# Attention and two expert layers in one kernel: new start places in SBUF for the Relu quarters and the weight slots

## The chip, the cores and the metric

One Trainium2 chip (trn2), one of its NeuronCores. The metric is the device time of one execution in microseconds (us); lower is better. "Place" means the byte at which an operand begins within a partition of SBUF, and "remainder" means that place modulo 256.

## What is computed

The reference runs linear attention with an RMS norm, then a dense layer of eight experts (every token goes through all eight, weighted by a balanced gate `P`), then a layer of eight experts in which each token goes to its best one:

```python
# dense expert layer, x: 2304 x 512, w1: 8 x 512 x 1024, w2: 8 x 1024 x 512
for e in range(E):
    h = np.maximum(x @ w1[e], 0.0)
    ye = h @ w2[e]
    out += P[:, e:e + 1] * ye
...
# routed expert layer
for e in range(E):
    mask = expert_idx == e
    h = np.maximum(x[mask] @ w1[e], 0.0)
    out[mask] = gate_w[mask, None] * (h @ w2[e])
```

## The kernel before, in words

Each fp32 matrix is held as a high and a low part in a reduced fp32 format (`F32R`). A product is three matmuls: high by high, high by low, low by high. Every matmul is one weight load of a 128x128 block (the stationary operand) and one pass of 256, 384 or 512 columns of the other operand (the moving one).

The dense layer is 24 steps: three blocks of 768 tokens times eight experts. The first matrix of a step is done with seven products of quarters in place of eight, in `fill` (L967): stationary is a weight quarter, moving is a quarter of the tokens (`xo`), 384 columns. That is 168 matmuls in each of the 24 steps, 4032 in all. Its results go through Relu and are kept as four "Relu quarters", each with a high and a low part of 1536 elements, named 11, 12, 21 and 22 and held in two tiles (in the profile all of them are called `d`).

The second matrix comes in two kinds. In steps 8 to 22 (`quick`) it is done with seven products of quarters, in `product` inside `down` (L1103): stationary is a Relu quarter, moving is a weight quarter, 256 columns; 252 matmuls in each of 15 steps, 3780 in all. In the steps 0 to 7 it is done in the plain way (L1316): the same stationary operands, moving weights of 512 columns, 1152 matmuls. The last step has its own code (L1344, 144 matmuls of 512 columns). The routed layer follows, with `f1` (L593, 256 columns), `f2` (L613, 512 columns, moving operand in the weight slots) and `single` (L1536, L1561, 512 columns).

Weights pass through four slots. Quarter number `g` of the whole program goes to slot `g % 4`, a high and a low tile of 4096 bytes. `slot_tiles` makes the two tiles anew for each quarter. They are filled in one of two ways: ScalarE casts the high part and GpSimd or VectorE subtracts it to make the low one (`prep`, `split_into`, L161, L166, L260), or SyncE fetches both parts from a copy in HBM (`fetch`, L279). Quarter `g + 3` is asked for while quarter `g` is being used (`ahead`).

The order of all work is written out by hand; nothing is scheduled by a planner. What the tiles' addresses are follows from their sizes and the order of the pools. Before the change all eight slot tiles begin at remainder 160, the token parts `xo` at 224, and the Relu tiles at 160; `place_h` moves the Relu quarters by 16 elements (64 bytes) in the fast steps, so that they begin at 224 there, and leaves them at 160 in the others. Quarters and rows within them are multiples of 256 bytes apart, so each matmul of a kind begins its two operands at the same two remainders: 160 (stationary) and 224 (moving) in `fill`, 224 and 160 in the fast steps' second matrix, 160 and 160 in the plain one and in `f2`, 160 and 96 in `f1` (its first call 224 and 160), 96 and 160 in `single`.

Of the kernel before, what the change touches and what calls it, by code (L numbers as in the profile page):

```python
# [9 lines left out]
F32R = mybir.dt.float32r  # L10
# [7 lines left out]
N, D, E, F = B * S, H * HD, 8, 1024  # L18
P = 128
# [21 lines left out]
def f32(ap):  # L41
    return ap.bitcast(F32)

@with_exitstack
def tile_linattn_moe_moe(ctx: ExitStack, tc: tile.TileContext, qT, k, v, g2, wg, w1a, w2a, emb, embT, tau, w1b, w2b, out):
# [4 lines left out]
    wp = ctx.enter_context(tc.tile_pool(name="w", bufs=1))  # L50
# [9 lines left out]
    def get(pool, shape, dtype, tag, bufs=1):  # L60
        if not ringed[0]:
            return pool.tile(shape, dtype, tag=tag, name=tag, bufs=bufs)
        if tag not in rings:
            rings[tag] = [[pool.tile(shape, dtype, tag=tag, name=tag, bufs=bufs) for _ in range(bufs)], 0]
        r = rings[tag]
        r[1] += 1
        return r[0][(r[1] - 1) % bufs]
# [84 lines left out]

    def split(raw, tag, eng=None, hi_eng=None):
        pool, name = places[tag]
        hi = get(pool, [P, 1024], F32R, name + "h")
        lo = get(pool, [P, 1024], F32R, name + "l")
        return split_into(raw, hi, lo, eng, hi_eng)

    def split_into(raw, hi, lo, eng=None, hi_eng=None):
        if hi_eng is None:  # L160
            nc.scalar.copy(hi, raw)  # L161
        else:
            hi_eng.tensor_copy(hi, raw)
        if eng is nc.gpsimd and dense[0]:
            for c in (slice(0, 512), slice(512, 1024)):
                eng.tensor_tensor(lo[:, c], raw[:, c], f32(hi[:, c]), ALU.subtract)  # L166
        else:
            (eng or nc.vector).tensor_tensor(lo, raw, f32(hi), ALU.subtract)
        return hi, lo
# [19 lines left out]
    def quick(s):  # L189
        return E <= s < NSTEP - 1  # L190
# [9 lines left out]
    for i, g in enumerate(plain):  # L200
        plain_load.setdefault(plain[i - 2] - 2 if i > 1 else base[E] - 4 + i, []).append(g)

    def slot_tiles(g):
        return (wp.tile([P, 1024], F32R, tag=f"g{g % 4}h", name="wh", bufs=1),
                wp.tile([P, 1024], F32R, tag=f"g{g % 4}l", name="wl", bufs=1))

    def load_quarter(s, name, t=None):
        t = t if t is not None else raw_tile()
# [34 lines left out]
    def prep(g, lo_eng=None):  # L243
        s, n = seq_of[g]

        def r(name):
            return raws[s, name]

        if g in plain_at:
            src = raws[g]  # L250
        elif n >= 7:
            src = r(W2ORDER[n - 7])
        else:
            if n == 2 and s == 0:
                sums(s)
            src = r(("w11", "w12", "s2", "w21", "w22", "s1", "w12")[n])
        hi, lo = parts[g] = slot_tiles(g)
        if s < E and lo_eng is None and g > 2:
            nc.scalar.copy(hi, src)  # L259
            after_two.append([2, lambda: nc.vector.tensor_tensor(lo, src, f32(hi), ALU.subtract)])  # L260
        else:
            split_into(src, hi, lo, lo_eng)
        if s < E and n in (2, 3):
            o, a, b = (r(i) for i in (("w21", "w11", "w21"), ("w12", "w12", "s2"))[n - 2])
            for c in (slice(0, 512), slice(512, 1024)):
                nc.gpsimd.tensor_tensor(o[:, c], a[:, c], b[:, c], ALU.subtract)
# [7 lines left out]
    def fetch(g):  # L274
        s, n = seq_of[g]
        parts[g] = slot_tiles(g)
        src = w1c[s % E, CACHED[n]] if n < 7 else w2c[s % E, DOWN[n - 7][1]].rearrange("i p f d -> i p (f d)")
        for i in range(2):
            nc.sync.dma_start(f32(parts[g][i]), src[i])  # L279
# [285 lines left out]
    xrow = qs.rearrange("p k n -> p (k n)")  # L565
    hq = {}
    groups = []
    HSHIFT = 16

    def place_h(o):  # L570
        for names, t in groups:
            for i, a in enumerate(names):
                hq[a] = [t[:, o + k * 4 * HB:o + (k + 1) * 4 * HB].rearrange("p (k n) -> p k n", k=4)
                         for k in (2 * i, 2 * i + 1)]

    def open_h(pool, names):
        groups.append((names, pool.tile([P, 16 * HB + HSHIFT], F32R, name="d" + names[0])))
        place_h(0)
# [620 lines left out]
    for s in range(NBK * E):  # L1199
# [28 lines left out]
                               (a + 20, lambda r: t_store(r, 0)), (a + 24, lambda r: t_store(r, 1))):  # L1228
                    thooks.setdefault(min(at_, 311), []).append(lambda f=f, r=r: f(r))
        fast = quick(s)  # L1230
        place_h(HSHIFT if fast else 0)
        if final:
            raw_n[0] = 0
        bank = {}
# [2 lines left out]
        for n in range(7):  # L1237
            g = base[s] + n
# [67 lines left out]
        elif not final:  # L1306
            ys = [ps_a() for _ in range(JT)]
            for m, q in enumerate(W2ORDER):
                g = base[s] + 7 + m
                wh, wl = parts[g]  # L1310
# [281 lines left out]
    def slot(f):  # L1592
        if f in steps:
            steps[f]()
        if f < 4:
            w2t.append(split(early2[f], f"w2{f}", nc.gpsimd))
        if f < 2:
            early_w1(f + 2, 1)
        if f == 1:
            for j in range(FT // 2):  # L1600
                early_w2(j, 1)
# [10 lines left out]
    def mid(f):  # L1612
        if f == 1:
            q_count()
        if f == 4:
            q_experts()
        kk = {1: 0, 3: 1}.get(f)
        if kk is not None:
            w1t[kk] = split(next1[kk], f"w1{kk}")
# [5 lines left out]
    def mid(f):  # L1625
        if f in (0, 2):
            kk = 3 - f // 2
            w1t[kk] = split(next1[kk], f"w1{kk}")
        if f == 3:
            q_slot()  # L1630
        if f == 6:
            q_cols(A16, R16, 0, NA)
# [166 lines left out]
```

## Time and profile before

| | |
|---|---|
| median of 3 runs | 1821.28 us (1820.44 to 1821.89) |
| the profiled execution | 1820.02 us |
| its span, first to last instruction | 1818.2 us |
| TensorE matmul busy (PE) | 1788.0 us, 98% |
| TensorE weight load busy (PEld) | 1698.3 us, 93% |
| VectorE, ScalarE, GpSimd busy (DVE, ACT, POOL) | 68%, 47%, 56% |
| granted TensorE clock | 0.995 of full, the 2.4 GHz level |

A row of instructions gives line, engine, operation, output and inputs by the program's names, the shape, a count, busy time and the mean duration of one. Matmuls overlap: a matmul's duration in the profile is longer than the time from its start to the next one's start. That second time, the spacing, is what adds up to the span.

### The profile page before, as it was taken

How to read it: one execution, taken by the hardware profiler on the slowest of the kernel's cores; microseconds unless marked ns; L12 is line 12 of the kernel's file. 1: busy time of each engine (PE TensorE's matmuls, PEld its weight loads, DVE VectorE, ACT ScalarE, POOL GpSimd, SP SyncE). 2: the span in 40 equal slices, each digit the busy share in tenths (PEclk: the TensorE clock that was granted, in tenths of full speed). 3: DMA queues.
4: the chain of work that ended last, by engine and by line, in shares of the span. 5: the costliest groups of instructions: out<-in, count | busy, mean ns of one | idle time of the engine just before them, and what ended most of it. 6: DMA issues, size and time to landing. Idle time of an engine off the chain costs nothing. (4 is left out here: it accounts for less than half of the span.)

```text
span 1818.2 us, 30973 instructions
## 1 busy us (share of the span) xinstructions
PE 1788.0 (98%) x11494; PEld 1698.3 (93%) x11494; DVE 1243.3 (68%) x2196; ACT 847.2 (47%) x1435; POOL 1021.7 (56%) x813
## 2 busy tenths in 40 slices
PE   7999999999999999999999999999999999999997
PEld 7989889989998999999999999999999998888996
DVE  3855686566656788866456778987567764877665
ACT  3645344344434634554444553454445433556443
POOL 1513378889879655764466475765466432543222
PEclk9999999999999999999999999999999999999998
DMA  9625367779768766556465766565555663588764
GB/s 298 224 70 203 106 227 277 259 268 342 277 233 280 273 212 211 197 186 223 167 217 190 247 220 237 179 216 208 181 198 186 228 212 102 188 304 287 232 227 157
DMA packets 185568, 397.73 MB, mean 219 GB/s; under 512 B 16448, under 2 KB 86592, under 8 KB 185408
## 3 DMA queue, kind: packets, MB, share of 16 engines
q1 hardware_dynamic: 179680, 378.33, 60.4%
q0 software_dynamic: 4000, 13.11, 2.1%
q10 hardware_dynamic: 1728, 4.23, 0.7%
q8 instruction: 92, 1.51, 0.3%
q14 instruction: 68, 0.56, 0.1%
HBM read 314.61 MB, written 81.00 MB: 218 GB/s over the span
## 5 line engine op out<-in xcount | busy, mean ns | idle before, releaser
L967 PE MATMUL A<-xo,wh 128*128 128x384 f32 x2688 | 687.8, 337 | 1.0 <-DVE u L955 0.4
L967 PEld LDWEIGHTS A<-xo,wh 128*128 128x128 f32 x2688 | 482.6, 188 | 3.2 <-DVE u L955 1.2
L967 PE MATMUL A<-xo,wl 128*128 128x384 f32 x1344 | 452.2, 336 | 1.8 <-POOL wl L166 1.4
L1103 PE MATMUL A<-wh,d 128*128 128x256 f32 x2520 | 447.7, 281 | 0.6 <-POOL d L1157 0.6
L166 POOL TENSOR_TENSOR wl<-raw,wh 128x512 fp32r<-128x512 f32 x180 | 254.4, 1435 | 285.4 <-ACT wh L161 129.0
L1103 PEld LDWEIGHTS A<-wh,d 128*128 128x128 f32 x2520 | 387.6, 190 | 0.8 <-POOL d L1157 0.8
L1103 PE MATMUL A<-wl,d 128*128 128x256 f32 x1260 | 353.7, 281 | 0.0
L967 PEld LDWEIGHTS A<-xo,wl 128*128 128x128 f32 x1344 | 252.6, 188 | 3.3 <-POOL wl L166 2.6
L1316 PE MATMUL A<-wh,d 128*128 128x512 f32 x768 | 243.8, 392 | 0.0
L1103 PEld LDWEIGHTS A<-wl,d 128*128 128x128 f32 x1260 | 236.5, 188 | 0.0
L952 DVE SCALAR_TENSOR_TENSOR d<-A,d 128x384 fp32r<-128x384 f32 x228 | 125.9, 553 | 160.4 <-ACT raw L1254 90.1
L166 POOL TENSOR_TENSOR wl<-rb,wh 128x512 fp32r<-128x512 f32 x92 | 129.3, 1426 | 161.4 <-ACT wh L161 150.2
L1316 PEld LDWEIGHTS A<-wh,d 128*128 128x128 f32 x768 | 144.2, 188 | 29.7 <-issue 0.3
L957 ACT ACTIVATE d<-A 128x384 fp32r<-128x384 f32 x132 | 65.4, 497 | 198.5 <-DVE A L955 196.2
L1316 PE MATMUL A<-wl,d 128*128 128x512 f32 x384 | 149.5, 389 | 0.0
L1250 ACT COPY qs<-A 128x384 f32<-128x384 f32 x96 | 45.5, 479 | 190.1 <-PE A L967 185.4
L161 ACT CAST wh<-raw 128x1024 fp32r<-128x1024 f32 x94 | 98.4, 1047 | 12.4 <-DMA raw<-in_w1a_dram 4.2
L260 DVE TENSOR_TENSOR wl<-raw,wh 128x1024 fp32r<-128x1024 f32 x45 | 70.3, 1564 | 36.4 <-ACT wh L259 25.8
L1153 POOL TENSOR_TENSOR d<-qs,d 128x384 fp32r<-128x384 f32 x60 | 64.8, 1111 | 48.0 <-ACT d L1151 48.0
L1316 PEld LDWEIGHTS A<-wl,d 128*128 128x128 f32 x384 | 72.2, 188 | 14.1
L955 DVE TENSOR_TENSOR A<-A,qs 128x384 f32<-128x384 f32 x132 | 73.6, 560 | 16.7 <-PE A L967 16.4
L1259 DVE TENSOR_TENSOR u<-A,qs 128x384 f32<-128x384 f32 x96 | 52.2, 554 | 32.0 <-PE A L967 31.9
(496 smaller groups left out, 3366.6 us busy)
## 6 DMA issues: line engine op xcount, KB each, us to landing
raw<-in_w1a_dram SPq DMA_DIRECT2D x64, 512.0 KB, 4.4
wh<-w1c SPq DMA_DIRECT2D x64, 512.0 KB, 4.9
wl<-w1c SPq DMA_DIRECT2D x64, 512.0 KB, 6.4
wh<-w2c SPq DMA_DIRECT2D x60, 512.0 KB, 5.1
wl<-w2c SPq DMA_DIRECT2D x60, 512.0 KB, 5.9
raw<-in_w2a_dram SPq DMA_DIRECT2D x51, 512.0 KB, 4.5
raw<-in_w1b_dram SPq DMA_DIRECT2D x48, 512.0 KB, 5.0
raw<-in_w2b_dram SPq DMA_DIRECT2D x48, 512.0 KB, 3.8
```

Of the source, the lines that this page charges most:

```text
L161: nc.scalar.copy(hi, raw)
L166: eng.tensor_tensor(lo[:, c], raw[:, c], f32(hi[:, c]), ALU.subtract)
L260: after_two.append([2, lambda: nc.vector.tensor_tensor(lo, src, f32(hi), ALU.subtract)])
L952: nc.vector.scalar_tensor_tensor(hl[:, i, :], src, 0.0, f32(hh[:, i, :]), ALU.max, ALU.subtract)
L955: nc.vector.tensor_tensor(dst, ps, u, ALU.add)
L957: nc.scalar.activation(hq[a][0][:, i, :], dst, AF.Relu)
L967: nc.tensor.matmul(ps[:, 0:HB], a[:, fs], bb[:, kk, :], start=(first and j == 0), stop=(j == 5), skip_group_check=True)
L1103: nc.tensor.matmul(o, a[:, f, ts_], bb[:, ds_], start=(m in first and j != 1 and i == 0), stop=(i == 11), skip_group_check=True)
L1153: nc.gpsimd.tensor_tensor(a12[1][:, i], qs[:, i], f32(a12[0][:, i]), ALU.subtract)
L1250: nc.scalar.copy(qs[:, i, :], p)
L1259: nc.vector.tensor_tensor(u3[:, i, :], p, qs[:, i, :], ALU.add)
L1316: nc.tensor.matmul(ys[j], a, bb[:, ds_], start=(m + ff + i == 0), stop=(m == 3 and ff == 1 and i == 2))
```

## The change

Three edits. (1) The four weight slots become four tiles that are made once, each of 2048 + 16 elements; the high part begins the tile, and the low part begins 0, 8, 4 or 16 elements (0, 32, 16, 64 bytes) behind the end of the high one. As a tile is now 64 bytes longer, the slots begin at remainders 160, 224, 32 and 96, and their low parts at 160, 0, 48 and 160. (2) In the fast step `s` the Relu quarters are placed `2 * (s - 8)` elements into their tiles, that is 0, 8, 16 ... 112 bytes, in place of 64 bytes in all of them. (3) The Relu tiles grow by 16 elements (64 bytes) to hold that; one of them stays at 160 and the other, which is laid out from the far end, comes to begin at 96. `split` takes the slots' parts directly for the second expert layer.

```diff
     def split(raw, tag, eng=None, hi_eng=None):
         pool, name = places[tag]
+        if pool is wp:
+            return split_into(raw, *slots[int(name[1])], eng, hi_eng)
...
+    slots = {}
+    LOW_AT = (0, 8, 4, 16)
+
     def slot_tiles(g):
-        return (wp.tile([P, 1024], F32R, tag=f"g{g % 4}h", name="wh", bufs=1),
-                wp.tile([P, 1024], F32R, tag=f"g{g % 4}l", name="wl", bufs=1))
+        if g % 4 not in slots:
+            o = 1024 + LOW_AT[g % 4]
+            t = wp.tile([P, 2048 + 16], F32R, name=f"g{g % 4}")
+            slots[g % 4] = t[:, 0:1024], t[:, o:o + 1024]
+        return slots[g % 4]
...
-    HSHIFT = 16
+    HSHIFT = 32
...
-        place_h(HSHIFT if fast else 0)
+        place_h(2 * (s - E) if fast else 0)
```

No instruction is added, removed or moved on any engine; lines move by 8. What differs in the program are addresses, the names of the slot tiles (now `g` for both parts), and which semaphores some instructions wait for. GpSimd, in a fast step's second matrix, before (`wl` and `wh` are a slot's parts, `rb` and `raw` hold plain weights, `d` is a Relu quarter):

```order
L166 TENSOR_TENSOR wl<-rb,wh 128x512 [waits DMAHW4_49,DMAHW6_49,PE_49,Activation_49]
L166 TENSOR_TENSOR wl<-rb,wh 128x512
L1273 TENSOR_TENSOR d_766<-u_518,d_766 128x384 [waits Activation_49] x2
L166 TENSOR_TENSOR wl<-raw,wh 128x512 [waits DMAHW1_49,PE_49,Activation_49]
L166 TENSOR_TENSOR wl<-raw,wh 128x512
```

and the same place after the change:

```order
L168 TENSOR_TENSOR g_566<-rb,g_566 128x512 [waits DMAHW5_49,DMAHW0_49,Activation_49]
L168 TENSOR_TENSOR g_566<-rb,g_566 128x512 [waits PE_49]
L1281 TENSOR_TENSOR d_756<-u_515,d_756 128x384 [waits Activation_49] x2
L168 TENSOR_TENSOR g_500<-raw,g_500 128x512 [waits DMAHW1_49,Activation_49]
L168 TENSOR_TENSOR g_500<-raw,g_500 128x512 [waits PE_49,Pool_49]
```

The wait for TensorE moves from the first half of a low part to the second half, as the halves are now tracked apart; the instructions and their order are the same.

## Rows read from the trace of the kernel before

**Rows 1.** The page, part 1, and the granted clock of part 2.
```profile
PE 1788.0 (98%) x11494; PEld 1698.3 (93%) x11494; DVE 1243.3 (68%) x2196; ACT 847.2 (47%) x1435; POOL 1021.7 (56%) x813
...
PEclk9999999999999999999999999999999999999998
```
**Rows 2.** Who waited for whom, TensorE: us in total, times, longest.
```profile
PE M L381 <- DMA v<-in_v_dram: 7.3, 2, 5.8
...
PE A L967 <- POOL wl L166: 1.4, 3, 0.8
...
PE A L1103 <- POOL d L1157: 0.6, 1, 0.6
```
**Rows 3.** The page, part 5, the three large matmul groups with `wh`.
```profile
L967 PE MATMUL A<-xo,wh 128*128 128x384 f32 x2688 | 687.8, 337 | 1.0 <-DVE u L955 0.4
...
L1103 PE MATMUL A<-wh,d 128*128 128x256 f32 x2520 | 447.7, 281 | 0.6 <-POOL d L1157 0.6
...
L1316 PE MATMUL A<-wh,d 128*128 128x512 f32 x768 | 243.8, 392 | 0.0
```
**Rows 4.** Timeline of TensorE in a fast step, 17 triples apart: start us, us.
```profile
868.86 0.40 PE L1103 MATMUL A<-wh,d 128*128 128x256 f32 x2
...
874.87 0.40 PE L1103 MATMUL A<-wh,d 128*128 128x256 f32 x2
```
**Rows 5.** Groups of TensorE, 912 to 941.4 us (second matrix, step 13).
```profile
L1103 PE MATMUL A<-wh,d 128*128 128x256 f32 x167 | 29.6, 281 | 0.0
L1103 PE MATMUL A<-wl,d 128*128 128x256 f32 x84 | 23.6, 281 | 0.0
```
**Rows 6.** Timeline of TensorE in step 21, around a small matmul group.
```profile
1397.93 0.28 PE L1103 MATMUL A<-wh,d 128*128 128x256 f32 x1
1398.06 0.46 PE L810 MATMUL M<-pG,pB 128*128 128x6 bf16 x12
1398.38 0.36 PE L1103 MATMUL A<-wh,d 128*128 128x256 f32 x1
```
**Rows 7.** Groups of TensorE, 1399.2 to 1405.3 us (step 21, after that group).
```profile
L1103 PE MATMUL A<-wh,d 128*128 128x256 f32 x38 | 6.5, 276 | 0.0
L1103 PE MATMUL A<-wl,d 128*128 128x256 f32 x19 | 5.2, 276 | 0.0
```
**Rows 8.** Timeline of TensorE there, 16 triples apart.
```profile
1399.61 0.28 PE L1103 MATMUL A<-wl,d 128*128 128x256 f32 x1
...
1405.05 0.28 PE L1103 MATMUL A<-wl,d 128*128 128x256 f32 x1
```
**Rows 9.** Groups of TensorE in `f1`, 1631 to 1642, then 1780 to 1795 us.
```profile
L593 PE MATMUL A<-xh,w13h 128*128 128x256 f32 x7 | 1.9, 276 | 0.0
...
L593 PE MATMUL A<-xh,w10h 128*128 128x256 f32 x8 | 2.2, 281 | 0.0
```
**Rows 10.** By line, whole span: duration ns min/median/max, first and last start us.
```profile
L967 PE MATMUL A<-xo,wl x1344: 332/336/445, 54.1 to 1502.1; 128*128 128x384 f32 x192
...
L1103 PE MATMUL A<-wl,d x1260: 276/281/283, 618.0 to 1472.9; 128*128 128x256 f32 x180
...
L1316 PE MATMUL A<-wl,d x384: 387/389/397, 96.2 to 587.6; 128*128 128x512 f32 x192
```
**Rows 11.** Groups of TensorE, 95.8 to 136 us (rows often broken).
```profile
L967 PE MATMUL A<-xo,wl 128*128 128x384 f32 x1 | 0.3, 338 | 0.0
```
**Rows 12.** By line, `single` (stationary at 96, moving at 160), and `f2` (160 and 160).
```profile
L1536 PE MATMUL A<-w10h,xh x4: 392/392/392, 1618.0 to 1657.2; 128*128 128x512 f32 x4
...
L1536 PE MATMUL A<-w10l,xh x4: 394/394/394, 1618.2 to 1657.4; 128*128 128x512 f32 x4
...
L1536 PE MATMUL A<-w10h,xl x4: 388/388/388, 1618.5 to 1657.7; 128*128 128x512 f32 x4
...
L613 PE MATMUL A<-g0l,hh x40: 389/389/398, 1557.7 to 1803.6; 128*128 128x512 f32 x40
```
**Rows 13.** Timeline of GpSimd in step 12, then of TensorE at the same place.
```profile
876.33 2.57 POOL L166 TENSOR_TENSOR wl<-rb,wh 128x512 fp32r<-128x512 f32 x2
...
874.04 0.28 PE L1103 MATMUL A<-wl,d 128*128 128x256 f32 x1
```
**Rows 14.** Timelines of GpSimd, then VectorE, end of step 15 and step 16.
```profile
1051.61 5.35 POOL L1157 TENSOR_TENSOR d<-raw,d 128x384 fp32r<-128x384 f32 x4
...
1070.39 0.56 DVE L952 SCALAR_TENSOR_TENSOR d<-A,d 128x384 fp32r<-128x384 f32 x1 [0.81 <-ACT raw L1254]
```
**Rows 15.** The page, part 6: fetches into the slots, KB each, us to landing.
```profile
wl<-w1c SPq DMA_DIRECT2D x64, 512.0 KB, 6.4
...
wl<-w2c SPq DMA_DIRECT2D x60, 512.0 KB, 5.9
```

## The prediction

> **What bounds the kernel now.** I read the page's busy times first. TensorE's matmuls are busy for 1788.0 of 1818.2 us and the clock is granted in full in every slice that counts [rows 1]; the other engines are well below. The waits of TensorE come next: the longest total is 7.3 us at the first loads, and the two largest inside the dense layer are 1.4 and 0.6 us [rows 2]. So there is no wait left from which a change of order could take much. What remains is how long one matmul takes, times their number. The matmul groups give the numbers [rows 3]: 4032 matmuls of 384 columns (2688 with `wh`, half as many with `wl`), 3780 of 256 columns in the fast steps, 1152 of 512 columns in the plain ones.
>
> A matmul's duration in these rows is not its cost; the spacing to the next start is. In a settled stretch of a fast step, 17 triples take 874.87 - 868.86 = 6.01 us, or 117.8 ns a matmul [rows 4], where the mean duration is 281 ns [rows 5]. Duration less spacing is 163 ns. I take this constant for the other settled stretches: 336 ns of duration at 384 columns is a spacing of 173 ns, and 389 ns at 512 columns is 226 ns [rows 10]. A nanosecond more or less in the duration is then a nanosecond of span for each matmul of that group.
>
> From 384 to 512 columns the duration grows by 53 ns, 0.414 ns a column, which is a cycle at 2.4 GHz (0.417 ns). At that rate 256, 384 and 512 columns are 106.7, 160.0 and 213.3 ns. So each matmul pays about 11, 13 and 13 ns beyond its columns. This extra is nearly the same for 384 and 512 columns, so it belongs to the one weight load that goes with each matmul and not to the columns. That is the only thing this change can touch.
>
> **Does it depend on the place?** The trace holds three hints.
> - At one shape, one line and one pair of remainders it takes two values: 281 ns in most fast products, 276 ns after a short group of other matmuls had broken the row [rows 6, 7]; the spacing there is 5.44 us over 48 matmuls, 113.3 ns [rows 8]. `f1` shows the same two values [rows 9]. Matmul and weight load thus settle into a fixed pattern, and there is more than one such pattern.
> - Where stationary and moving operand stand in another relation, the pattern is another: `single` (96 and 160) repeats 392, 394, 388, a mean of 391.3 ns, against 389 ns for `f2` (160 and 160), both at 512 columns [rows 12]. That is 2.3 ns more.
> - While a row is unsettled, durations spread from 332 to 338 ns at 384 columns (the 445 is the break itself) and from 387 to 397 ns at 512 [rows 10, 11].
>
> So a weight load's extra can be moved, by some nanoseconds either way, and the place is one of the things that go with it.
>
> The Trainium skill speaks against this: TensorE: Matmul & The Clock Gate, Part 2 (Step-by-step), says that the engine reads the streamed operand and the weights through two independent ports, so that loading the next weights takes nothing from the running matmul; then no place could matter. The trace does not agree with it as it stands, since the 384-column matmul is spaced by 173 ns and not by its 160. By the rule the sum below would be zero.
>
> **What the change touches.** No instruction is added or moved. Counted by remainder of stationary less remainder of moving operand, the pair changes for: 2624 of the 4032 matmuls of `fill` (slot 0 stays at 160 in both parts, slot 3 in its low part); 3720 of the 3780 of the fast products; and 864 + 320 + 96 + 32 = 1312 of 512 columns (plain steps, `f2` as executed, last step, `single`'s second half). `f1` and `single`'s first half keep theirs. In a slot whose low part stands elsewhere than its high one, the three matmuls of a triple also no longer share one pair.
>
> **The prices**, each with both ends.
> - Fill, 2624 matmuls. The present pair costs 336 ns; unsettled rows run from 332 to 338 [rows 10, 11]. I take no change, as 336 lies in the spread, nearer its upper end. Ends: 2624 x -4 ns = -10.5 us and 2624 x +2 ns = +5.2 us.
> - Fast products, 3720 matmuls. They now pay 11.1 ns beyond their columns, where the two other shapes pay 13.3 (173.3 - 160.0). A pair picked without regard to the pattern should cost what the others cost, 2.2 ns more: +8.2 us. Lower end: the other pattern at 276 ns, a spacing 4.4 ns lower (113.3 against 117.8) [rows 4, 8], -16.4 us. Upper end: 2.2 + 2.3 = 4.5 ns, with the price of the odd relation of `single` on top [rows 12], +16.7 us.
> - Matmuls of 512 columns, 1312. I take the one row that shows another pair at this shape, +2.3 ns [rows 12]: +3.0 us. Ends: 387 ns gives -2.6 us, 397 ns gives +10.5 us [rows 10].
> - Waits. On GpSimd the wait for TensorE moves to the second half of a low part; in the tightest place it starts at 876.33 + 1.28 = 877.6 us, while the last matmul it has to see was issued near 874.04 us and ended by 874.4 us [rows 13]: 3 us of cover, in 35 places. VectorE's Relu low parts now wait for GpSimd's last split of the step before, which ends at 1051.61 + 5.35 = 1057.0 us, 13 us ahead of the tightest of them [rows 14]. Both cost nothing; behind each stand only instructions that TensorE asks for later. If the cover were gone, TensorE would be late at L967 by the difference, as it is for 1.4 us now [rows 2].
> - Fetches into slots that begin at other remainders. They land 6.4 and 5.9 us after issue [rows 15] and are asked for some two and a half quarters of 24 x 173 ns = 4.2 us ahead, 10.4 us. A landing would have to grow by 4 us to be seen. Nothing.
> - The persistent slot tiles remove no instruction. Nothing; covered by the same rows as the waits.
>
> **The sum**: 0 + 8.2 + 3.0 = +11.2 us on the profiled execution's 1820.0 us, 1831.2 us. The median of the runs stands 1.3 us above that execution, so I forecast 1832 us, slower by 0.6%. What a measurement here can tell from no change is about 0.2%, 3.6 us.
>
> **Rivals.**
> 1. *Faster: the fast products fall into the 276 ns pattern.* It decides in `product` (L1103): the extra is moved below 11 ns when the weight load and the columns of the running matmul stop meeting. For it: the pattern exists at this very line, and holds for dozens of matmuls once reached [rows 7 to 9]. Against it: with one fixed pair, each undisturbed step enters the 281 ns one again after the fill, and with changing pairs in a triple there is less to hold a pattern. All 3720 in it give -16.4 + 3.0 = -13.4 us, 1808 us in terms of the median. With a share x of them in it, 3720 x (2.2 - 6.6 x) + 3.0 us falls below -3.6 us from x = 0.6 on. Chance 0.25, with gains in the fill counted here too.
> 2. *No change: places do not matter, only how a row was entered.* For it: the two values at one pair. Against it: `single`'s 391.3 ns and its pattern of three values. Then the time stays at 1821 us. By the skill's rule on the two ports, too, it would. Chance 0.13, which includes gains and losses that cancel.
> 3. *Much slower: places that are no multiple of 32 bytes cost the weight load itself.* Nothing of the large groups in the trace stands at such a place, so no row shows it; I bound it by the upper ends above: 5.2 + 16.7 + 10.5 = +32.4 us, 1854 us. It lies in the forecast's side, with a chance of 0.1 of the 0.62 there.
>
> That the change does nothing but rename is ruled out by the addresses: the pair of remainders differs for 7656 matmuls.
>
> **The numbers.** Slower 0.62 (forecast and rival 3), same 0.13, faster 0.25. The range goes from 1806, just beyond all fast products at 276 ns, to 1850, short of the sum of all upper ends; outside I leave 0.1 at the top and 0.08 at the bottom. The side of the forecast alone runs from 1825 to 1850.
>
> **What would show it.** By step, the fast products' mean duration: 283 to 285 ns on average with a spread over the 15 steps means the forecast, 276 in most of them rival 1, 281 in all of them rival 2. In the fill, slot 0's triples should stay at 336 and the others scatter about it. The 512-column rows should read 391 or more in slots 1 to 3. Waits of TensorE should stay as they are; if they grow by more than 2 us, my reading of the cover is wrong. If the fill's mean falls to 332, that would make the forecast wrong from the side that I priced at nothing.

## The result, and the profile after

The kernel after the change takes 1831.26 us (median of 4 runs, 1830.23 to 1831.57), the kernel before, beside it, 1820.86 us (4 runs, 1820.03 to 1821.89). The ratio is 1.0056 [1.0038, 1.0073]: slower by 0.6%, 10.4 us. Span of the profiled execution: 1828.3 us, against 1818.2 before.

The page of the kernel after, busy time and granted clock, to be laid beside [rows 1]:

```profile
PE 1800.6 (98%) x11494; PEld 1705.1 (93%) x11494; DVE 1247.2 (68%) x2196; ACT 847.3 (46%) x1435; POOL 1008.1 (55%) x813
...
PEclk9999999999999999999999999999999999999999
```

TensorE is busy for 12.6 us more with the same 11494 matmuls at the same clock, and idle for 2.5 us less (27.7 us of its span, 30.2 before). Who waited for whom on TensorE, the counterpart of [rows 2]:

```profile
PE M L389 <- DMA v<-in_v_dram: 6.5, 2, 5.8
...
PE A L975 <- POOL g L168: 1.1, 2, 0.6
```

So the time did not go into waits: the one on GpSimd is 1.1 us where it was 1.4. It went into the matmuls. By line, the counterpart of [rows 10] and [rows 9] (duration in ns, min/median/max; high and low slot parts are one group here, as both are called `g`; L975 is the fill, L1111 the fast products, L1324 the plain ones, L601 and L621 are `f1` and `f2`; the last line is `f1` before the change):

```profile
L975 PE MATMUL A<-xo,g x4032: 331/337/448, 52.8 to 1513.0; 128*128 128x384 f32 x192
...
L1111 PE MATMUL A<-g,d x3780: 274/280/388, 622.5 to 1483.7; 128*128 128x256 f32 x199
...
L1324 PE MATMUL A<-g,d x1152: 387/393/505, 95.1 to 592.9; 128*128 128x512 f32 x192
...
L621 PE MATMUL A<-g,hh x320: 387/393/483, 1566.8 to 1816.6; 128*128 128x512 f32 x160
...
L601 PE MATMUL A<-xh,w13h x72: 276/276/281, 1579.7 to 1804.1; 128*128 128x256 f32 x72
...
L593 PE MATMUL A<-xh,w13h x72: 276/281/281, 1569.3 to 1793.9; 128*128 128x256 f32 x72
```

Medians of the fill and of the 512-column lines rise, the fast products' does not, and `f1` falls from 281 to 276 ns. What adds up to the span is the spacing from start to start. I summed it over every matmul of a line, in the trace of before and of five kernels, of which the last four are described below (us in all; in brackets the mean ns of one, without breaks, that is spacings in which other work or a wait falls):

| group | before | after | slots alone | Relu alone | one place a slot | couple (248, 224) |
|---|---|---|---|---|---|---|
| fill, 4032 | 709.0 (173.4) | 713.7 (175.0) | 714.1 (175.0) | 707.8 (173.4) | 715.4 (175.0) | 708.2 (173.4) |
| fast, 3780 | 445.4 (117.5) | 447.9 (118.2) | 446.1 (117.7) | 448.2 (118.1) | 446.2 (117.7) | 431.6 (113.7) |
| plain, 1152 | 264.4 (227.4) | 269.0 (231.5) | 268.8 (231.4) | 266.9 (229.6) | 268.2 (230.8) | 264.4 (227.4) |
| `f1`, 960 | 114.9 (116.8) | 112.7 (114.4) | 112.3 (114.0) | 115.0 (117.0) | 112.6 (114.2) | 115.2 (116.9) |
| `f2`, 480 | 110.9 (227.2) | 111.9 (231.0) | 112.4 (230.9) | 110.4 (227.1) | 113.1 (231.5) | 110.5 (227.1) |
| last step, 144 | 34.4 | 34.5 | 34.5 | 34.5 | 34.5 | 34.3 |
| all other | 121.7 | 121.4 | 124.4 | 119.3 | 119.8 | 122.2 |

Before to after: +4.7 fill, +2.5 fast, +4.6 plain, +1.0 `f2`, +0.1 last, -2.2 `f1`, -0.3 other: +10.4 us, where the span grew by 10.1.

Within the fill the loss follows the slot. Windows of the kernel after in one fill of step 10, the fill's line alone, each from the first start of one slot's product to the first start of the next (24 matmuls; the first figure behind the window is its length in us, and the counts in brackets take in neighbours that overlap): slots 2, 3, 0 and 1.

```profile
719.33:723.53 4.20, 4.20 (x26) 4.20 (x26) 1.00 0.86 323
723.53:727.74 4.21, 4.21 (x26) 4.21 (x25) 1.00 0.92 281
727.74:731.90 4.16, 4.16 (x26) 4.16 (x26) 1.00 0.29 110
731.90:736.14 4.24, 4.24 (x26) 4.24 (x26) 1.00 0.00 0
```

Divided by 24: 175.0, 175.4, 173.3 and 176.7 ns. Slot 0, which kept its place, kept its spacing. The DMA share (the column ahead of GB/s) is 0.29 in slot 0's window and 0.00 in the slowest, so it does not follow the traffic.

### The profile page after: what moved, and what is told of

Read it like the earlier page. It is cut to its first block, busy times and chain, and to the rows that moved or that the text cites. A ratio compares the mean times of both kernels' runs of the same rounds, so it can differ in the third digit from the quotient of the medians.

```text
span 1828.3 us, 30891 instructions
## 1 busy us (share of the span) xinstructions
PE 1800.6 (98%) x11494; PEld 1705.1 (93%) x11494; DVE 1247.2 (68%) x2196; ACT 847.3 (46%) x1435; POOL 1008.1 (55%) x813
## 3 DMA queue, kind: packets, MB, share of 16 engines
q10 hardware_dynamic: 1728, 4.23, 0.6%
## 4 chain that ended last, share of the span: by engine, by line
PE 92%; DVE 3%; DMA 1%; ACT 1%; issue 1%; POOL 1%; SPq 0%; DVEq 0%; ACTq 0%; POOLq 0%
PE A L975 36%; PE A L1111 24%; PE A L1324 15%; PE A L601 5%; PE A L621 5%; PE A L1352 2%; PE M L430 1%; PE A L1544 1%; PE M L398 1%; PE M L422 0%; PE M L389 0%; PE M L634 0%; PE A L398 0%; DMA w1c<-g 0%; DMA xg<-x2d,idx 0%
## 5 line engine op out<-in xcount | busy, mean ns | idle before, releaser
L975 PE MATMUL A<-xo,g 128*128 128x384 f32 x4032 | 718.7, 338 | 1.7 <-POOL g L168 1.1
L975 PEld LDWEIGHTS A<-xo,g 128*128 128x128 f32 x4032 | 703.0, 188 | 5.0 <-POOL g L168 2.0
L1111 PE MATMUL A<-g,d 128*128 128x256 f32 x3780 | 450.8, 281 | 0.0
L1111 PEld LDWEIGHTS A<-g,d 128*128 128x128 f32 x3780 | 449.2, 188 | 0.5 <-POOL d L1165 0.2
L168 POOL TENSOR_TENSOR g<-raw,g 128x512 fp32r<-128x512 f32 x180 | 251.6, 1420 | 297.3 <-ACT g L163 245.1
L1324 PE MATMUL A<-g,d 128*128 128x512 f32 x1152 | 273.4, 395 | 0.0
L1324 PEld LDWEIGHTS A<-g,d 128*128 128x128 f32 x1152 | 214.6, 188 | 48.3 <-issue 0.3
L168 POOL TENSOR_TENSOR g<-rb,g 128x512 fp32r<-128x512 f32 x92 | 128.3, 1417 | 162.1 <-ACT g L163 161.8
L163 ACT CAST g<-raw 128x1024 fp32r<-128x1024 f32 x140 | 146.4, 1046 | 12.8 <-DMA raw<-in_w1a_dram 3.2
L621 PE MATMUL A<-g,hh 128*128 128x512 f32 x320 | 101.0, 396 | 0.0
L268 DVE TENSOR_TENSOR g<-raw,g 128x1024 fp32r<-128x1024 f32 x45 | 73.0, 1623 | 36.3 <-ACT g L267 30.0
L170 DVE TENSOR_TENSOR g<-raw,g 128x1024 fp32r<-128x1024 f32 x44 | 56.6, 1292 | 19.7 <-ACT g L163 16.0
L621 PEld LDWEIGHTS A<-g,hh 128*128 128x128 f32 x320 | 58.5, 188 | 12.2 <-DVE g L170 0.2
L267 ACT CAST g<-raw 128x1024 fp32r<-128x1024 f32 x45 | 47.1, 1046 | 48.0 <-PE A L1324 25.4
```

The source lines that it names most:

```text
L621: nc.tensor.matmul(ps, a[:, ts_], bb[:, ds_], start=(i == 0), stop=(i == 3 * FT - 1))
L975: nc.tensor.matmul(ps[:, 0:HB], a[:, fs], bb[:, kk, :], start=(first and j == 0), stop=(j == 5), skip_group_check=True)
L1111: nc.tensor.matmul(o, a[:, f, ts_], bb[:, ds_], start=(m in first and j != 1 and i == 0), stop=(i == 11), skip_group_check=True)
L1324: nc.tensor.matmul(ys[j], a, bb[:, ds_], start=(m + ff + i == 0), stop=(m == 3 and ff == 1 and i == 2))
```

## The experiments

In what follows a pair is (remainder of the stationary operand, remainder of the moving one), and a couple is the remainders of the two Relu tiles. The theories of the first four runs: **P**, a matmul's spacing is set by its pair; **W**, the loss comes from tiles that are made once and the waits that go with them; **M**, it comes from a triple whose high and low parts stand at different places. Later runs add **H**, the spacing depends also on what ran before, and **D**, only the difference of the two remainders counts.

**The slots alone**: the change without its two Relu edits.

```diff
-    HSHIFT = 32
+    HSHIFT = 16
...
-        place_h(2 * (s - E) if fast else 0)
+        place_h(HSHIFT if fast else 0)
```

> The four slots stand as in the change, the Relu quarters stay 64 bytes into their tiles in every fast step as before. Theory P (the spacing of a matmul goes with the remainders of its two operands): the fill keeps what it costs in the changed kernel, slot 0 at 173.4 ns and slots 1 to 3 at 175 to 177 ns, +5 us in all; the 512-column matmuls of slots 1 to 3 are 3 to 6 ns slower, +5 us; the fast products lie between -2 and +4 us. Sum about +8 to +10 us, 1829 to 1831 us. Theory W (the tiles that are made once change the waits): the same time, but TensorE's waits grow by several us.

Measured 1830.4 us (1830.06 to 1831.9), ratio 1.0061 [1.0047, 1.0074]. The slots alone lose as much as the whole change, in fill (+5.1 us), plain (+4.4) and `f2` (+1.5). On top of them the Relu edits of the change add 1.8 us of fast products and next to nothing else.

**The Relu places alone**: the kernel before with the two Relu edits of the change.

```diff
-    HSHIFT = 16
+    HSHIFT = 32
...
-        place_h(HSHIFT if fast else 0)
+        place_h(2 * (s - E) if fast else 0)
```

> The slots stay as before, the Relu quarters take the 15 places of the change. Theory P: fill unchanged at 173.3 ns; the plain steps' matmuls of the Relu tile that moved to remainder 96 are slower by about 2 to 4 ns, +2 us; fast products differ from step to step between 113 and 120 ns, mean near 118, about +1 us. Sum +1 to +5 us, 1822 to 1826 us. Theory W: no change, 1821 us.

Measured 1826.69 us, with a wide spread (1821.0 to 1830.63), ratio 1.0046 [1.0032, 1.0059], just above the 1822 to 1826 of P. The profiled execution took 1821.0 us, the least of the five; in it fast costs +2.8 us, plain +2.5 (the second Relu tile stands at 96 there: its products take 231.8 ns, those of the first, still at 160, 227.4), and fill, `f2` and the rest give 4.1 us back. The same kernel was run again to see where the spread comes from:

> The kernel with the Relu places alone once more, for a second profile: its times spread from 1821.0 to 1830.6 us and the profile at hand is of the fastest run. Theory H, a product's spacing hangs on what stood before it: the spread then sits in matmul groups that settle otherwise from run to run, and a profile of a run above 1824 us shows it as more spacing in plain (above 229.6 ns) or fast (above 118.1 ns) by the run's excess. Rival: the spread is outside the matmuls of the two layers, those groups stay within 0.5 us of the first profile and the rest grows.

Measured 1826.29 us (1822.27 to 1826.86), ratio 1.0026 [1.0015, 1.0037]; the profiled execution took 1822.64 us, again one of the lowest, so it decides neither way. Its matmul groups agree with the first profile within 0.5 us. The two profiles account for spans that are 1.0 and 2.7 us longer than before; what makes most runs of this kernel another 4 to 10 us longer stays open. One thing the two profiles do show: the same program does not always settle alike. The fast products of step 9 take 117.4 ns in the one and 116.6 in the other, those of step 19 take 116.1 and 117.4.

**Tiles made once, all places as before**: the slots' new code with `LOW_AT = (0, 0, 0, 0)` and tiles of 2048 elements, Relu as before.

> The slots are made once, as in the change, but every part stands at remainder 160 as before, and the Relu quarters too. Theory P: 1821 us, each group's durations as before (336, 281, 389 ns). Theory W: slower by 3 us or more, with waits of TensorE to show for it.

Measured 1820.52 us, ratio 1.0001 [0.9992, 1.001]. Its groups, from the page:

```profile
L975 PE MATMUL A<-xo,g 128*128 128x384 f32 x4032 | 712.6, 337 | 2.0 <-POOL g L168 1.4
...
L1111 PE MATMUL A<-g,d 128*128 128x256 f32 x3780 | 447.8, 281 | 0.6 <-POOL d L1165 0.6
...
L1324 PE MATMUL A<-g,d 128*128 128x512 f32 x1152 | 268.8, 391 | 0.0
```

and the same lines of the kernel after:

```profile
L975 PE MATMUL A<-xo,g 128*128 128x384 f32 x4032 | 718.7, 338 | 1.7 <-POOL g L168 1.1
...
L1111 PE MATMUL A<-g,d 128*128 128x256 f32 x3780 | 450.8, 281 | 0.0
...
L1324 PE MATMUL A<-g,d 128*128 128x512 f32 x1152 | 273.4, 395 | 0.0
```

W falls: TensorE waits as before and the time is that of before. This kernel and the one with the slots alone have the same instructions and the same slot code, and differ in `LOW_AT` and the tiles' length, that is in addresses only: 1820.5 against 1830.4 us. That is the cleanest single reading here.

**One place for high and low of a slot**: as the slots alone, with `LOW_AT = (0, 0, 0, 0)` and tiles of 2048 + 16 elements; slots at 160, 224, 32, 96.

> Slots at the remainders 160, 224, 32 and 96, but high and low part of a slot at the same one; Relu quarters as before. Theory P: slots 1 to 3 are slower than slot 0 in the fill and at 512 columns, as in the first of these kernels; +6 to +10 us. Theory M (it is the two different places within a triple of high and low that cost): a slot whose parts share a place settles as slot 0 does, fill 173.4 ns in all four, 1821 us give or take 3.

Measured 1829.52 us (1828.61 to 1830.47), ratio 1.0054 [1.0041, 1.0068]: the loss is there without any mixed triple, so M falls. Windows of its plain products in one step, 36 matmuls each, at the pairs (160, 160), (160, 224), (160, 32):

```profile
306.18:314.35 8.17, 8.17 (x36) 6.76 (x37) 1.00 1.04 376
314.35:322.61 8.26, 8.26 (x38) 6.76 (x36) 1.00 1.06 352
322.61:330.97 8.36, 8.36 (x37) 6.78 (x36) 1.00 0.95 313
```

That is 226.9, 229.4 and 232.2 ns; on the mean of the kernel 227.9, 229.4, 232.4, and 233.3 for (160, 96). The fill at (160, 224), (224, 224), (32, 224), (96, 224) takes 173.5, 174.4, 176.0, 176.0 ns. So far P. But the fast products at (224, 160), the pair of all of them in the kernel before, take 113.8 ns here and 117.8 there. P alone can't be all of it: here products at other pairs run in between, there all of them are at this one.

**Relu quarters at 96.** In the run with the Relu places alone the pair (96, 160) had 113.3 ns in all three products that stood there, all in step 8. If P holds, putting all fast products there should gain. H is the rival.

```diff
-    HSHIFT = 16
+    HSHIFT = 48
+    PLACE = ((0, 32), (48, 16))
...
-    def place_h(o):
-        for names, t in groups:
+    def place_h(fast):
+        for (names, t), o in zip(groups, PLACE[fast]):
...
-        place_h(HSHIFT if fast else 0)
+        place_h(fast)
```

> The kernel before with one edit: the two Relu quarters of every fast step stand at remainder 96 of 256 (before: 224 bytes), slots stay at 160. Theory P, the pair of remainders sets the spacing: the pair (96, 160) ran at 113.3 ns in the run with the Relu places alone, so the 3780 fast products fall from 117.5 ns to 113.3 to 114 ns, 13 to 16 us less, total 1804 to 1807 us; fill, plain and the rest as before. Rival H, a product keeps the spacing that its group entered with: the fast products stay at 117.5 to 118 ns and the total is 1820 us.

Measured 1820.49 us, ratio 1.0008 [0.9999, 1.0017]; the 3774 fast matmuls outside breaks take 117.8 ns, at the pair that had shown 113.3. P in its simple form falls.

**A scan of the fill's place**: slots at 160, 192, 232 and 56, both parts alike.

> One tile of slots, made once, with the four slots at remainders 160, 192, 232 and 56, high and low part alike; Relu as before. A scan of the fill's stationary remainder against the same moving 224. Theory P: each slot's fill triples have a spacing of their own between 169.5 and 179.5 ns per product, slot 0 at 173.4 as before; the total is 1812 to 1835 us by what the three new pairs turn out to be. Rival H: all four slots within 1 ns of one another in the fill.

Measured 1826.89 us (one run). Fill by slot: 173.6, 176.0, 173.7, 173.5 ns. No place is better for the fill than that of the kernel before, and its pairs do differ. The fast products show something else: windows of step 8, 36 matmuls each, moving operand at 56, 160, 192, 232 (stationary always 224):

```profile
621.70:626.02 4.32, 4.32 (x36) 4.32 (x37) 1.00 0.67 204
626.02:630.12 4.10, 4.10 (x38) 4.10 (x37) 1.00 1.04 408
630.12:634.38 4.26, 4.26 (x39) 4.26 (x37) 1.00 0.94 349
634.38:638.60 4.22, 4.22 (x38) 4.22 (x37) 1.00 0.20 73
```

120.0, 113.9, 118.3, 117.2 ns: behind products at 56, the old pair (224, 160) is in the short pattern (113.3 ns, but for the first few) again.

**All of the left side 128 bytes further**: four slot tiles made once behind a gap of 128 bytes, so slots at 32; Relu at 224 in the fast steps and 32 in the plain ones.

> One tile of slots, made once, with every slot and all else on the left side 128 bytes further: slots at remainder 32, Relu quarters of the fast steps still at 224, of the plain steps at 32. Stationary less moving is then -64 (mod 256: 192) in the fast products, the same difference as in the pair (96, 160). Theory P in the form that only the difference of the remainders counts: fast products 113.3 to 114 ns, total 1805 to 1810 us. P in the form that each remainder counts by itself: 117.5 to 118.5 ns as for the pair (224, 32) in the run with one place for each slot; fill at the pair (32, 224) 176.0 ns, so total 1828 to 1834 us.

Measured 1829.21 us (one run). Fill at (32, 224) 175.8 ns, as in the run above; fast at (224, 32) 117.8; plain at (32, 32) 227.4, just as at (160, 160). So the plain products take the same time at 32 as at 160, the two places tried where both operands share a remainder. The fast products speak against D, but do not settle it, as (96, 160), with the same difference as (224, 32), has shown both 113.3 and 117.8 ns. The fill adds something: from step 9 to 15 whole fills alternate, 174.7 ns in the odd steps and 176.7 in the even ones, at one pair and behind fast products at one pair, and from step 16 on to 19 the other way round. So the pair of the product just before does not decide alone either.

**Fifteen couples.** Is it then the products before that decide? Each fast step gets another couple of remainders for its two Relu tiles. `PLACE` becomes a list of fifteen, `HSHIFT` 64.

```diff
...
+    AT = ((248, 96), (248, 184), (248, 248), (96, 248), (160, 96), (248, 160), (248, 224), (96, 160),
+          (32, 96), (224, 96), (0, 96), (56, 96), (248, 120), (192, 248), (248, 32))
+    PLACE = [(0, 48)] + [((a - 160) % 256 // 4, (b - 224) % 256 // 4) for a, b in AT]
...
-        place_h(HSHIFT if fast else 0)
+        place_h(s - E + 1 if fast else 0)
```

> The kernel before, where the two Relu tiles of each of the 15 fast steps get another couple of remainders (first tile, second tile), slots at 160: (248, 96), (248, 184), (248, 248), (96, 248), (160, 96), (248, 160), (248, 224), (96, 160), (32, 96), (224, 96), (0, 96), (56, 96), (248, 120), (192, 248), (248, 32). A step's seven products take first, second, first, first, second, second, first tile. Theory H, a product's spacing is set by its own pair and by the products before it: (160, 96) and (248, 184) come out as in the run with the Relu places alone, 117.1 and 116.0 ns on the mean of a step, as those had the same neighbours; a product at 96 has 113.3 ns behind one at 160 and 117 to 120 ns behind some others; at least one couple has over half of its products at 113.3 to 114 ns. Rival P, a product's own pair alone, with a scatter from run to run: 248 runs at 113.5 to 114.4 ns in whatever couple it stands, 96 at one value throughout. Total 1810 to 1822 us by either.

Measured 1817.34 us (one run). Windows of its fast line, 36 matmuls each: the first two products of step 8 (248, then 96), the first two of step 12 (160, then 96) and the first three of step 17 (224, then 96, then 224):

```profile
619.45:623.56 4.11, 4.11 (x37) 4.11 (x37) 1.00 0.75 255
623.56:627.64 4.08, 4.08 (x39) 4.08 (x37) 1.00 0.93 330
...
852.47:856.78 4.31, 4.31 (x36) 4.31 (x37) 1.00 0.77 253
856.78:860.86 4.08, 4.08 (x38) 4.08 (x37) 1.00 1.00 387
...
1146.41:1150.64 4.23, 4.23 (x36) 4.23 (x37) 1.00 0.70 213
1150.64:1154.88 4.24, 4.24 (x38) 4.24 (x37) 1.00 1.01 404
1154.88:1158.96 4.08, 4.08 (x38) 4.08 (x37) 1.00 0.89 314
```

A product at 96 takes 4.08 us (113.3 ns) behind one at 248 or at 160, and 4.24 us (117.8 ns) behind one at 224 that itself had 4.23. P falls and H fits: several pairs, (224, 160) and (96, 160) among them, have two settled patterns, and what ran before goes with which one a product takes: the step at (160, 96) came out at 117.1 ns, as H had it, that at (248, 184) at 116.3 for 116.0. The pair (160, 160) had 119.8 to 120.0 ns in all its products of this run. 248 as first tile led into the short pattern straight from the fill, in every step that began with it (114.2 to 114.4 ns in the first product, 113.3 behind its first few matmuls). It does not keep that whatever stands before it: 248 had 116.7 ns behind 160, and up to 117.7 in products into which other matmuls fell. The couples (248, 96) and (248, 224) had 113.46 ns on the mean of all seven products, against 117.8 in an unbroken step before.

**These two couples in all fast steps.** `AT` becomes 15 times (248, 224), then 15 times (248, 96).

> The kernel before with the couple (248, 224) in all 15 fast steps: the first Relu tile of a fast step at remainder 248, the second at 224; slots at 160, plain steps at 160. Theory H: as in the one step that had this couple (113.46 ns on the mean of its seven products), so 113.5 ns against 117.5 ns, 3780 x -4.0 ns = -15 us, total 1804 to 1807 us; the rest as before. Rival: the 113.3 ns of that step came of what the step before it left, then the fast products are back at 117.5 to 118 ns and the total is 1819 to 1821 us.

> The same with the couple (248, 96), which also ran at 113.46 ns in its one step. Theory H: 1804 to 1807 us, with the products at 96 at 113.3 ns throughout, though 96 alone held 117.8 ns in all fast steps. Rival: 117.5 to 118 ns and 1819 to 1821 us.

Measured 1806.83 us (1805.63 to 1809.19), ratio 0.9927 [0.9913, 0.9941], and 1806.69 us, ratio 0.9924 [0.991, 0.9938]: faster than the kernel before by 13.5 and 13.7 us, inside the range of H. Of the kernel with (248, 224), page and fast line:

```profile
PE 1773.7 (98%) x11494; PEld 1684.2 (93%) x11494; DVE 1242.2 (69%) x2196; ACT 846.1 (47%) x1435; POOL 1016.0 (56%) x813
...
L1105 PE MATMUL A<-wh,d 128*128 128x256 f32 x2520 | 433.5, 277 | 0.9 <-POOL d L1159 0.9
...
L1105 PE MATMUL A<-wh,d x2520: 276/276/391, 617.4 to 1458.7; 128*128 128x256 f32 x194
```

The fast group falls from 447.7 to 433.5 us of busy time [rows 3], its spacing sum by 13.8 us, and no other row of the table moves by more than 0.8 us. Thirteen of the 15 steps sit at 113.5 to 113.6 ns; where the pattern was left, in step 20, it came back with the next step (116.0, then 113.9 ns).

**Does the difference of the two remainders decide?** In the last run the routed layer's `f1` gets the difference of the pair (248, 160), 88, by token parts that stand 24 bytes lower.

```diff
-        return get(xcp, [P, KC, BLK], F32R, "xh"), get(xcp, [P, KC, BLK], F32R, "xl")
+        return [get(xcp, [P, KC * BLK + 64], F32R, a)[:, 58:58 + KC * BLK].rearrange("p (k n) -> p k n", k=KC)
+                for a in ("xh", "xl")]
```

> The kernel with the couple (248, 224), and the token parts of the routed layer 24 bytes less in remainder, so that 1632 of the 1728 matmuls of the routed layer's first matrix go from the pair (160, 96) to (160, 72). Stationary less moving is then 88, as in the pair (248, 160), which holds 113.3 ns behind whatever stood before it in six of seven couples. Theory D, it is the difference of the two remainders that counts: this group falls from 116.9 to 113.3 to 114 ns, 1632 x -3.2 ns = -5 us, total 1800 to 1803 us. Rival, the remainder of each operand counts by itself: anything from 113.3 to 120 ns, so -6 to +5 us, with the group's old 117 ns (1806 to 1808 us) as likely as any.

Measured 1808.18 us (1806.1 to 1810.44), ratio 0.9932 [0.9919, 0.9946], against 0.9927 without this edit; these two can't be told apart. The group can: of the 1632 matmuls in the program, 864 are executed, and these go to 120.0 ns, which takes the sum of `f1` from 115.2 to 117.7 us. By line, with the edit:

```profile
L595 PE MATMUL A<-xh,w13h x72: 280/282/283, 1556.1 to 1783.2; 128*128 128x256 f32 x72
```

where the kernel without it has a median of 281. All nine calls took 120 ns, the seven behind `f2` and the two behind `single`, while (248, 160), with the same difference, was never settled there. So the difference of the remainders is not the whole rule either, though some pairs that share one agree, as (160, 160) and (224, 224) at 119.4 to 120.1 ns. I have a table of pairs and couples, not a formula.

## Why the prediction was right, point by point

The direction was right, and so was the mechanism in the large: the places change the spacing of the matmuls, with no change in waits. That the total came within 1 us (1832.0 forecast, 1831.26 measured) is luck. The forecast put 8.2 of 11.2 us on the fast products; the runs put 2.5 of 10.4 there, and most on the fill and the matmuls of 512 columns. Three of its terms were mis-sized and one was missing; they cancelled.

- **Fill, priced at 0: measured +4.7 us**, near the upper end of +5.2. The step that failed is "I take no change, as 336 lies in the spread": the present pair is one of the best for the fill. Six other places were tried for both parts of a slot (224, 32, 96, 192, 232, 56): 173.5 to 176.0 ns on the mean, none below the 173.4 of the old one. That slot 0 would stay was right; that the others would scatter about it was not, as all three went up (175.0 to 176.6 ns).
- **Fast products, priced at +8.2 us: measured +2.5.** The step was that a pair picked at random pays the 13.3 ns of the other shapes. It pays 11.5: 118.2 less 106.7 ns. By step the durations were 279.4 to 283.7 ns, not the 283 to 285 that I gave as the mark of the forecast. 117.5 ns was already an average value for this shape, with 113.3 and 120 on its two sides.
- **Matmuls of 512 columns, priced at +3.0 us: measured +5.7** (4.6 + 1.0 + 0.1). The step was to take 2.3 ns from `single`; over the 864 changed plain matmuls it is 4.6 us / 864 = 5.3 ns. The kernel before has equal remainders in these, which is the best case seen (227.4 ns, at 160 and at 32); the runs showed 229 to 235 ns for unequal ones.
- **`f1`, which "keeps its pair", so no term: measured -2.2 us.** Its pair is the same and its spacing is 114.4 where it was 116.8. Before, six of its seven calls behind `f2` took 117.8 ns and the two behind `single` 113.7; after, those behind `f2` took 113.4 to 114.5. The slots alone do the same (112.3 us), the Relu places alone do not (115.0), so it goes with the places of the slots, which `f2` reads just before; no run moved those of `f2` alone. I had read two values at one pair in [rows 7, 9] and used that for the fast products only.
- **Waits, fetches, tiles made once, at 0:** right; the run with the tiles made once and the places kept shows it at 1.0001.
- **"It belongs to the one weight load":** not shown. No run here tells whether what a matmul pays beyond its columns is the weight load's or its own, and the sum does not need it.

The rivals. *Places do not matter* falls with two kernels that differ in addresses alone and by 9.9 us. The Trainium skill, TensorE: Matmul & The Clock Gate, Part 2 (Step-by-step), says that the streamed operand and the weights come over two independent read ports, so that loading the next weights does not steal read bandwidth from the running matmul. The prediction drew from it that no place could matter, and the measurement decides against that; whether the ports have a part in it no run here shows. *Much slower at places that are no multiple of 32 bytes* falls as well: 248 is none, and the best kernel stands there. *Faster, the fast products fall into the 276 ns pattern* didn't happen with this change, which left every fast step between 117.3 and 118.9 ns, but it names what could be had: priced at -16.4 us, it measured -13.8 with the couple (248, 224).

## What to carry to other kernels

When TensorE is busy throughout, sum the spacing from start to start by line and divide by the count: a few nanoseconds per matmul of excess over the columns are worth as much as a wait, and addresses alone move them. Try places with one scan, a different one in each step of one kernel, and read them in order, since a place is good or bad together with what runs just before it. Before moving operands that already stand well, see what value the present place has among the possible ones: two of the three groups here were already at the best that any run showed.

## What the runs showed of the hardware

- At 256 columns two settled spacings are by far the commonest, and shared by many pairs: 113.3 and 117.8 ns; others are 116.7, 118.3 and 120.0. At the 2.4 GHz level three matmuls at 113.3, 117.8 and 120.0 ns are 816, 848 and 864 cycles. The fill's best, 173.3 ns, is 416 cycles for one matmul, and the plain products settle at 226.7 ns, 544 cycles, where both remainders are 160.
- The same pair has more than one settled spacing. (224, 160) holds 117.8 ns behind the fill and 113.3 behind products at 248; (96, 160) likewise. At 384 columns (32, 224) showed it too: 173.3, 174.7 and 176.7 ns in the kernel with all slots at 32.
- At 512 columns equal remainders took 227.4 ns (at 160 and at 32) and unequal ones 229 to 235 ns.
- What in the engine makes these patterns is not shown by any run here.
